# Attention, DFT and MLP on one core: two output rows of the second product kept in PSUM, half-array masks, one small add on ScalarE, and a new instruction order

## The chip, the core and the metric

One core of a Trainium2 chip runs the whole program. The metric is the device time of one execution in microseconds. The kernel before takes 950.18 us, the median of three runs (949.14 to 953.03).

## What is computed

The sizes are 4 batches, 12 heads, 448 positions, head size 64, model width 768 and hidden width 3072.

```python
scores = scale * q @ k.T                       # per batch and head, 448 x 448
scores = where(column > row, -1e9, scores)
attn = exp(scores - max(scores))
attn = attn / (sum(attn) + 1e-09)
x = attn @ v                                   # heads side by side: 4 x 448 x 768
u = x + real(fft(fft(x, axis=1), axis=2))
un = (u - mean(u)) / sqrt(var(u) + 1e-06)      # over the 768
out = u + maximum(un @ w_ch1, 0.0) @ w_ch2
```

## The kernel before

**Two-part numbers.** To keep accuracy, an operand of a product is cut into a high and a low part in float32r; a product is then three matmuls: high by high, high by low, low by high. One engine casts the high part (`copy`, line 333 or 335), another subtracts it for the low part (lines 430, 810, 866, 904, 1014, 1107).

**Attention** (`attend`) runs over 24 pairs of heads, two heads side by side in the 128 partitions. For each pair there are three score pieces: blocks of rows 0 and 1 together, block 2, and the tails of 64 rows of both heads. TensorE first writes the mask into the bank (line 447: an identity `idb` times a triangle `mkb`, both bfloat16, whole array), then adds the scores (line 455). The scores of the two heads use the upper and the lower 64 rows of the array, into the banks `sc` and `sd`. The score is kept negated, so VectorE's minimum (line 467) is the maximum, and ScalarE takes the exponential and its sum (line 471). VectorE adds 1e-9 to the seven sums (line 479) and takes the reciprocal (line 483); GpSimd or ScalarE normalise (lines 490 and 492); TensorE transposes (line 503) and multiplies with `v` on column halves of the array (line 529).

**Folding, DFT and normalisation** (`fold`, `dft`) follow for each batch, on all engines.

**The MLP** takes the 1792 rows in two passes (`g`) of 896 rows, which are 7 blocks of 128 (`k`). Each pass has 12 chunks (`c`) of 256 hidden columns. `f1` makes the first product of a chunk in four quarters. A chunk is slow (8 products of quarters) or, from `C_FAST` on and in all of the second pass, fast (Winograd's 7 products, with sums and differences made by VectorE and GpSimd, and banks copied to `c` on the way). From `C_FAST` on, the cut weights of the first pass are stored in DRAM and loaded again in the second (`kept`). `f2` makes the second product. In the first pass each block `k` and half `n` of 384 columns is a tile `o2` of six matmuls in a bank of its own (line 1218); VectorE adds it to `acc` in SBUF (line 1167), which ends with 14 adds a chunk.

**Order.** A planner (`Plan`) writes the order of every engine before the program is built. Each unit has an engine or a choice of engines, a cost, and a priority; the constants at the top (`SPLIT_AT`, `NORM_AT`, `W_LEAD`, `MIX_LEAD` and so on) are leads in units of a thousand per head pair or chunk. The unit that can start first by the planner's clock comes next. The 8 PSUM banks are one pool; `BANKS` gives each kind of tile a reserve and a limit. The hardware then runs each engine's list in that order and waits on semaphores.

Of the kernel before, what the change touches and what calls it, by code (L numbers as in the profile page):

```python
# [23 lines left out]
R = 112  # L24
# [11 lines left out]
BANKS = dict(sc=(1, 3), sd=(1, 2), pt=(1, 3), x=(1, 2), ay=(1, 3), an=(1, 1), at=(1, 5), h=(0, 5), o2=(0, 5))  # L36
# [28 lines left out]
CW = 128 + 192  # L65
# [5 lines left out]
GRP = [(0, 113), (113, 112), (225, 111), (336, 112)]  # L71


class Plan:
# [11 lines left out]
    def add(self, eng, cost, prio, fn, rd=(), wr=(), phase=None):  # L86
# [5 lines left out]
        for x in set(z[:2] for z in (*rd, *wr)):  # L92
# [3 lines left out]
            n=n, engs=dict(zip(eng, cost)) if many else {eng: cost}, many=many, prio=prio, fn=fn, deps=deps, phase=phase,  # L96
            new=sorted({z[:2] for z in wr if z[0] in self.bufs}, key=str)))

    def order(self):
# [74 lines left out]
        now = {"V": None, "G": None}  # L174

        def takes(n, e, t):
# [11 lines left out]
        while len(seq) < len(units):  # L188
            best = None
            for e, cand in pool.items():  # L190
                for n in cand:
# [71 lines left out]
def tile_kernel(ctx, tc, qk, vv, w1, w2, cc, cd, cs, out):  # L263
# [7 lines left out]
        "cst": ("const", [128, CW], F32, 1), "idb": ("const", [128, 128], BF16, 1),  # L271
        "mkb": ("const", [128, CW - 128], BF16, 1),  "eps": ("const", [128, 4], F32, 1), "pw": ("const", [128, 4], F32, 1),
# [21 lines left out]
        "h": ("P", [128, 512], F32, 1), "o2": ("P", [128, 512], F32, 1),  # L294
# [21 lines left out]
    def dve(n, rate=0.96):  # L316
        return 69 + n / rate
# [33 lines left out]
    def consts():  # L351
# [1041 lines left out]
```

## Time and profile before

| | before |
|---|---|
| median of 3 runs | 950.18 us |
| profiled execution | 950.98 us, span 949.2 us |
| PE busy | 904.6 us (95%), 5636 matmuls |
| DVE busy | 856.9 us (90%), 1455 instructions |
| ACT busy | 544.4 us (57%), 1300 instructions |
| POOL busy | 502.4 us (53%), 523 instructions |
| DMA | 165.84 MB |

PE is TensorE's matmuls, DVE VectorE, ACT ScalarE, POOL GpSimd. The stages show in what each engine does over the span: attention and DFT up to some 240 us, a change-over to 295, the first MLP pass to 645, the second to the end. A matmul's end is modelled in this profile, so that one which streams for 0.17 us is shown with 0.34; starts are what to measure between. A fast chunk of the first product begins where `t2`, `t3` and `t4` first appear, from 397 us on.

### The profile page before, as it was taken

To read this page: it belongs to the slowest core of one execution; us is meant where nothing else is said; L and a number is where in the kernel's file an instruction comes from. 1 tells how busy PE (TensorE), PEld (TensorE's weight loads), DVE (VectorE), ACT (ScalarE), POOL (GpSimd) and SP (SyncE) were. 2 spreads that over 40 slices of the span, in tenths; PEclk is the share of its full clock that TensorE was granted. 3 is DMA by queue.
4 is the path that set the end of the run, shared out by engine and by line. 5 is a ranking of instruction groups with operands and counts; after the bars stand their busy time and mean duration, and the time that the engine had idled before them with its cause. 6 is when DMAs were issued, how large, how long until landed. Compare 5 with 4: busy or idle time off the path is not lost.

```text
span 949.2 us, 16148 instructions
## 1 busy us (share of the span) xinstructions
PE 904.6 (95%) x5636; PEld 806.7 (85%) x5636; DVE 856.9 (90%) x1455; ACT 544.4 (57%) x1300; POOL 502.4 (53%) x523
## 2 busy tenths in 40 slices
PE   7999999999799999999999998989999999999997
PEld 4667668777689999988989887988989999999996
DVE  6889999998997787999998899989999999999998
ACT  6999898988644545545444446645554444434441
POOL 4798698884742122443342338775765333333331
PEclk9999999999899999999999999999999999999999
DMA  7634624616578556758696568654114444444303
GB/s 276 215 98 165 179 83 133 166 41 193 143 217 316 200 200 237 243 192 287 242 320 252 206 225 300 184 203 168 68 38 146 148 128 118 139 134 144 124 1 116
DMA packets 67537, 165.84 MB, mean 175 GB/s; under 512 B 18976, under 2 KB 31904, under 8 KB 67360
## 3 DMA queue, kind: packets, MB, share of 16 engines
q1 hardware_dynamic: 67456, 164.82, 52.5%
q8 instruction: 44, 0.72, 0.3%
q14 instruction: 37, 0.30, 0.1%
HBM read 112.89 MB, written 54.74 MB: 177 GB/s over the span
## 4 chain that ended last, share of the span: by engine, by line
PE 55%; DVE 25%; ACT 7%; issue 6%; POOL 5%; DMA 2%; SPq 0%; DVEq 0%; POOLq 0%; ACTq 0%
PE h L977 20%; PE o L1179 14%; PE o L1218 8%; PE x L529 4%; DVE acc L1167 4%; PE pt L503 3%; PE sc L455 3%; DVE w L761 3%; DVE w L751 2%; DVE w L810 2%; ACT p L471 2%; DVE ws L823 2%; DVE w L757 1%; DVE hl L1014 1%; DVE mn L467 1%
## 5 line engine op out<-in xcount | busy, mean ns | idle before, releaser
L1167 DVE TENSOR_TENSOR acc<-o,acc 128x384 f32<-128x384 f32 x444 | 231.1, 548 | 27.7 <-PE o L1218 19.1
L1218 PE MATMUL o<-w2h,hh 128*128 128x384 f32 x336 | 113.6, 338 | 2.1 <-DVE acc L1167 2.1
L1218 PE MATMUL o<-w2l,hh 128*128 128x384 f32 x336 | 113.9, 339 | 1.4 <-POOL w2l L778 1.3
L1218 PE MATMUL o<-w2h,hl 128*128 128x384 f32 x336 | 113.4, 338 | 0.0
L778 POOL TENSOR_TENSOR w2l<-w,w2h 128x768 fp32r<-128x768 f32 x24 | 49.6, 2070 | 78.5 <-ACT w2h L774 71.5
L492 POOL TENSOR_TENSOR p<-p,ri 128x128 f32<-128x128 f32 (+3 forms) x113 | 79.1, 729 | 21.9 <-DVE ri L483 18.1
L810 POOL TENSOR_TENSOR w<-w,w 128x384 fp32r<-128x384 f32 x30 | 36.1, 1205 | 66.5 <-ACT w L333 65.5
L977 PE MATMUL h<-u11h,w 128*128 128x448 f32 x174 | 64.9, 379 | 3.0 <-ACT u11h L333 3.0
L1179 PE MATMUL o<-w2l,hl 128*128 128x384 f32 x288 | 63.6, 340 | 4.1 <-DVE acc L1167 4.0
L1218 PEld LDWEIGHTS o<-w2h,hh 128*128 128x128 f32 x336 | 63.5, 189 | 4.6 <-DVE acc L1167 2.8
L1218 PEld LDWEIGHTS o<-w2l,hh 128*128 128x128 f32 x336 | 63.4, 189 | 4.4 <-POOL w2l L778 2.4
L977 PE MATMUL h<-u22h,w 128*128 128x448 f32 x174 | 63.1, 370 | 3.2 <-DVE c L1050 3.2
L1179 PE MATMUL o<-w2h,hh 128*128 128x384 f32 x288 | 65.2, 339 | 0.8 <-DVE acc L1167 0.8
L333 ACT COPY c<-h 128x448 f32<-128x448 f32 x57 | 30.1, 529 | 59.2 <-POOL w L877 25.4
L977 PE MATMUL h<-u12h,w 128*128 128x448 f32 x174 | 63.7, 368 | 0.0
L1218 PEld LDWEIGHTS o<-w2h,hl 128*128 128x128 f32 x336 | 63.5, 189 | 0.0
L977 PE MATMUL h<-u21h,w 128*128 128x448 f32 x174 | 63.1, 367 | 0.0
L503 PE MATMUL pt<-cst,p 128*128 128x128 f32 (+1 forms) x384 | 56.9, 281 | 2.6 <-ACT p L490 1.9
L1179 PEld LDWEIGHTS o<-w2l,hl 128*128 128x128 f32 x288 | 51.6, 188 | 8.0 <-DVE acc L1167 6.1
L503 PEld LDWEIGHTS pt<-cst,p 128*128 128x128 f32 (+1 forms) x384 | 41.4, 139 | 16.9 <-issue 5.7
L877 POOL TENSOR_TENSOR w<-w 128x384 f32<-128x384 f32 x15 | 19.3, 1290 | 68.6 <-issue 59.7
L999 ACT ACTIVATE c<-c 128x448 f32<-128x448 f32 x36 | 20.8, 579 | 59.3 <-DVE c L1050 59.3
(212 smaller groups left out, 3006.6 us busy)
## 6 DMA issues: line engine op xcount, KB each, us to landing
w<-in_w_dram SPq DMA_DIRECT2D x48, 768.0 KB, 5.0
wp<-w SPq DMA_DIRECT2D x49, 384.0 KB, 3.7
w<-wp SPq DMA_DIRECT2D x49, 384.0 KB, 3.1
wf<-w SPq DMA_DIRECT2D x34, 384.0 KB, 2.7
w<-wf SPq DMA_DIRECT2D x17, 768.0 KB, 4.8
raw<-in_qk_dram SPq DMA_DIRECT2D x23, 480.0 KB, 3.9
us<-und SPq DMA_DIRECT2D x45, 224.0 KB, 4.0
v<-in_vv_dram SPq DMA_DIRECT2D x24, 256.0 KB, 3.1
```

What stands on the lines that cost most here:

```text
L333: nc.scalar.copy(out=out, in_=in_)
L455: nc.tensor.matmul(out=T[ps][:, at[r]:at[r] + n], lhsT=T[a][s, q0:q0 + 128], rhs=T[c][s, 0:n], start=False, stop=y == len(rows) - 1 and z ...
L492: nc.gpsimd.tensor_tensor(out=x, in0=x, in1=z.to_broadcast([128, KE[r]]), op=ALU.mult)
L503: nc.tensor.transpose(T[ps][0:m, 128 * k:128 * k + 128], T[pb][:, PO[r] + 128 * c:PO[r] + 128 * c + m], T["cst", 0][:, 0:128])
L529: nc.tensor.matmul(out=T[xps][64 * h:64 * h + 64, q0:q0 + w], lhsT=T[v][0:kk, c, h * D:(h + 1) * D], rhs=T[src][0:kk, s0 + h * sd:s0 + h * ...
L761: nc.vector.scalar_tensor_tensor(out=T[w32], in0=T[w32], scalar=3, in1=T[w][:, :, 1], op0=ALU.logical_shift_left, op1=ALU.bitwise_or)
L778: nc.gpsimd.tensor_tensor(out=T[wl], in0=T[w32].bitcast(F32), in1=T[wh], op=ALU.subtract)
L810: (nc.gpsimd if eng == "G" else nc.vector).tensor_tensor(out=T[z][:, 1], in0=src(), in1=T[z][:, 0], op=ALU.subtract)
L977: nc.tensor.matmul(out=T[ps][:, 0:S], lhsT=a[:, t], rhs=x[:, t], start=start and k == 0, stop=stop and k == 8, skip_group_check=True)
L1167: nc.vector.tensor_tensor(out=x, in0=T[ps][:, 0:384], in1=x, op=ALU.add)
L1179: nc.tensor.matmul(out=T[ps][:, 0:384], lhsT=hpart(j, h, a)[:, k * 128:k * 128 + 128], rhs=T[z][:, 384 * b:384 * b + 384], start=start and ...
L1218: nc.tensor.matmul(out=T[ps][:, 0:384], lhsT=T[a][:, m, k * 128:(k + 1) * 128], rhs=w[:, sl], start=(m == 0 and z == 0), stop=(m == 1 and ...
```

## The change

1. **Rows in PSUM.** From chunk 3 of the first pass on, the blocks `k` = 0 and 1 of the second product are not added to `acc` chunk by chunk. They accumulate over nine chunks in three banks, `ra` (block 0, columns 0 to 511), `rc` (block 1, the same columns) and `rb` (columns 512 to 767 of both). After chunk 11 four adds bring them to `acc`.
2. **Half-array masks.** `idb` and `mkb` go; the constants come as bfloat16 bits within the `cst` load, which grows from 320 to 384 columns. For the score pieces of two heads a mask is two products on row halves, of 128 and of 64 columns, each for `sc` and `sd`. A tail's mask stays one product on the whole array.
3. **1e-9 on ScalarE** instead of VectorE.
4. **The planner** adds a price (`TURN`) when TensorE goes from whole-array work (F) to row halves (R) or column halves (C) or back, and has other prices for VectorE and GpSimd in SBUF at the same time (`BOTH`, with `T` for VectorE's double-rate operations).
5. **Constants**: fast chunks begin at 6 instead of 5, tables load from the third head pair on, and most leads are new.

```diff
-SPLIT_AT, FOLD_AT = -509, 5113
-DFT_AT, DFT_STEP = (4036, 3873, 3298, 3640), (77, 105, 133, 132)
-W_LEAD, F2_LAG = 809, 561
-BANKS = dict(sc=(1, 3), ..., h=(0, 5), o2=(0, 5))
+SPLIT_AT, FOLD_AT = -803, 5113
+DFT_AT, DFT_STEP = (4120, 3839, 3298, 3640), (77, 105, 166, 132)
+W_LEAD, F2_LAG = 783, 604
+BANKS = dict(sc=(1, 3), ..., h=(0, 5), o2=(0, 5), ra=(0, 1), rb=(0, 1), rc=(0, 1))
-C_FROM, W_FROM, N_WARM = 0, 8, 11
-N_W1, N_C, N_WS, C_FAST, C_MIX = 7, 3, 3, 5, 7
-MIX_LEAD, FILL_LEAD = -94, 417
-LATER = dict(S=-1500, V=-248, G=-847)
-NORM_AT, TR_AT = 1675, 1894
+C_FROM, W_FROM, N_WARM = 2, 8, 11
+N_W1, N_C, N_WS, C_FAST, C_MIX = 7, 3, 3, 6, 7
+C_RES = 3
+MIX_LEAD, FILL_LEAD = 48, 267
+LATER = dict(S=-1406, V=-248, G=-851)
+NORM_AT, TR_AT = 1514, 1343
-BOTH = dict(V=0.42, G=0.72)
+TURN = dict(FF=0, RR=0, CC=0, FR=92, RF=92, FC=45, CF=45, CR=45, RC=45)
+BOTH = dict(V=0.45, T=0.18, G=0.74)
...
@@ Plan.order
+                    if e == "PE":
+                        t += TURN[array, u["use"]]
                     key = (t, u["prio"], n)
...
@@ consts
-            copy(eng, T["mkb", 0], T["cst", 0][:, 128:CW])
...
-            copy(eng, T["idb", 0], T["cst", 0][:, 0:128])
...
@@ attend
-                for ps in banks:
-                    for y, r in enumerate(rows):
-                        e, m0, mw = at[r] + KE[r], 128 if tail else 0, 64 if tail else 128
-                        nc.tensor.matmul(
-                            out=T[ps][:, e - mw:e], lhsT=T["idb", 0], rhs=T["mkb", 0][:, m0:m0 + mw], start=y == 0, stop=False,
-                            skip_group_check=True)
+                cb = T["cst", 0][:, 128:CW].bitcast(BF16)
+                idb, mk = cb[:, 0:128], cb[:, 128:512]
+                for y, r in enumerate(rows):
+                    e = at[r] + KE[r]
+                    for w, a, m0 in ((64, idb, 128),) if tail else ((128, mk[:, 256:384], 0), (64, mk[:, 192:320], 128)):
+                        for h, ps in enumerate(banks):
+                            s = slice(0, 128) if tail else slice(64 * h, 64 * h + 64)
+                            nc.tensor.matmul(
+                                out=T[ps][:, e - w:e], lhsT=a[s], rhs=mk[s, m0:m0 + w], start=y == 0 and m0 == (128 if tail else 0),
+                                stop=False, skip_group_check=True)
...
-            nc.vector.tensor_scalar(out=T[ri], in0=T[sm], scalar1=1e-9, scalar2=None, op0=ALU.add)
+            nc.scalar.activation(out=T[ri], in_=T[sm], func=ACTF.Copy, bias=1e-9)
...
@@ f2, before the loop over the two halves n
+            if k < 2 and c >= C_RES:
+                r, half = ("ra", "rc")[k], "rb"
...
+                    for m in range(2):
+                        wh, wl = T["w2h", (j, m)], T["w2l", (j, m)]
+                        for z, (a, w) in enumerate(((hh, wh), (hh, wl), (hl, wh))):
+                            first = m == 0 and z == 0 and c == C_RES
+                            last = m == 1 and z == 2 and c == NCH - 1
+                            for ps, c0, d0, cw, own in ((r, 0, 0, 512, True), (half, 512, 256 * k, 256, k == 0)):
+                                nc.tensor.matmul(
+                                    out=T[ps][:, d0:d0 + cw], lhsT=T[a][:, m, k * 128:(k + 1) * 128], rhs=w[:, c0:c0 + cw],
+                                    start=first and own, stop=last, skip_group_check=True)
...
+                if c == NCH - 1 and k == 1:
...
+                                nc.vector.tensor_tensor(out=x, in0=T[ps][:, d0:d0 + cw], in1=x, op=ALU.add)
...
+                continue
```

What that does to the order is shown at three places. The first is TensorE's list at chunk 3 of the first pass, where the second product comes to block 0. Before (`o_5276` is the tile of the block's first half, `h` a tile of the first product):

```order
L1218 MATMUL o_5276<-w2h,hh 128x384
L1218 MATMUL o_5276<-w2l,hh 128x384
L1218 MATMUL o_5276<-w2h,hl 128x384
L1218 MATMUL o_5276<-w2h,hh 128x384
L1218 MATMUL o_5276<-w2l,hh 128x384
L1218 MATMUL o_5276<-w2h,hl 128x384
L977 MATMUL h<-u11h,w_5047 128x448
L977 MATMUL h<-u11l,w_5047 128x448
```

Now, at the same place of the work:

```order
L1233 MATMUL ra<-w2h,hh 128x512
L1233 MATMUL rb<-w2h,hh 128x256
L1233 MATMUL ra<-w2l,hh 128x512
L1233 MATMUL rb<-w2l,hh 128x256
L1233 MATMUL ra<-w2h,hl 128x512
L1233 MATMUL rb<-w2h,hl 128x256
L1233 MATMUL ra<-w2h,hh 128x512
L1233 MATMUL rb<-w2h,hh 128x256
```

The block is one unit of twelve matmuls into two banks that stay taken, where it was two units of six, each in a bank that an add set free again.

The second place is TensorE's list in attention, from the product with `v` to the scores of rows 0 and 1 of a head pair. Before (LDWEIGHTS loads the stationary operand; score rows carry it within):

```order
L529 MATMUL x<-pa,v 64x64 x2
L447 LDWEIGHTS idb
L447 MATMUL sc<-mkb,idb 128x128
L447 LDWEIGHTS idb
L447 MATMUL sc<-mkb,idb 128x128
L447 LDWEIGHTS idb
L447 MATMUL sd<-mkb,idb 128x128
L447 LDWEIGHTS idb
L447 MATMUL sd<-mkb,idb 128x128
L455 MATMUL sc<-kh,qh 128x128
```

Now, for such a pair:

```order
L541 MATMUL x<-pg,v 64x256 x2
L458 LDWEIGHTS cst
L458 MATMUL sc<-cst 128x128
L458 LDWEIGHTS cst
L458 MATMUL sd<-cst 128x128
L458 LDWEIGHTS cst
L458 MATMUL sc<-cst 128x64
L458 LDWEIGHTS cst
L458 MATMUL sd<-cst 128x64
```

The masks alternate between the two banks and are twice as many; 168 mask matmuls become 312. Over the whole list the neighbours of different array use change: F to R or back from 91 to 40, F to C or back from 119 to 56, R to C or back from 5 to 52.

The third is VectorE's list at the add of 1e-9 of a head pair (`un` is the normalisation of a DFT row, `mn` the minimum of a score piece). Before:

```order
L425 SCALAR_TENSOR_TENSOR ql<-raw,qh 128x512
L683 TENSOR_SCALAR un<-u,mv,rs 112x768
L479 TENSOR_SCALAR ri<-sum 128x7
L467 TENSOR_REDUCE mn<-sc 128x1
L483 RECIPROCAL ri<-ri 128x7
```

Now the add is in ScalarE's list, between an exponential, copies and normalisations:

```order
L483 ACTIVATE p,sum<-sd,mn 128x384
L347 COPY pg<-pt 128x512
L491 ACTIVATE ri<-sum 128x7
L483 ACTIVATE p,sum<-sc,mn 128x448
L347 COPY pg<-pt 128x512
L502 ACTIVATE p<-p,ri 128x448
```

VectorE keeps the reciprocal. Other work changes engine too. To VectorE go 9 scalings of `q` (9 to 18), 5 casts of `k` (11 to 16) and 10 copies to `xt` (4 to 14), all from ScalarE, which in turn does 70 normalisations instead of 55 and GpSimd 98 instead of 113. In all, VectorE's `acc` adds go from 444 to 412, TensorE's matmuls of 448 columns in the first product are 9 more, and one more chunk's second-pass weights are cut anew.

## Rows read from the trace of the kernel before

**Rows 1.** Busy time by stretch: length; PE, PEld, DVE, ACT, POOL (instructions); clock, DMA.

```profile
20.00:235.00 215.00, 209.16 (x1902) 154.04 (x1904) 191.94 (x393) 192.46 (x597) 173.53 (x220) 1.00 0.45 139
295.00:395.00 100.00, 100.00 (x535) 95.83 (x534) 83.10 (x128) 47.99 (x73) 27.31 (x19) 1.00 0.64 221
395.00:645.10 250.10, 234.76 (x1224) 219.96 (x1223) 235.77 (x333) 126.33 (x222) 125.91 (x92) 0.99 0.70 241
645.10:700.00 54.90, 52.14 (x272) 48.38 (x271) 52.59 (x89) 28.79 (x68) 42.02 (x39) 1.00 0.27 93
```

**Rows 2.** The chain that ended last, at 306 us: start, length, what.

```profile
306.13 3.71 PE h L977 x18
309.85 2.08 PE o L1218 x12
```

**Rows 3.** Busy time by stretch of line 977 alone, then of line 1218.

```profile
395.00:645.10 250.10, 122.50 (x527) 97.39 (x527) 0.99 0.70 241
...
395.00:645.10 250.10, 133.85 (x697) 123.66 (x696) 0.99 0.70 241
```

**Rows 4.** TensorE's waits, 395 to 645 us: total, times, longest.

```profile
PE h L977 <- ACT c L333: 9.5, 7, 2.8
...
PE o L1218 <- DVE acc L1167: 2.1, 2, 1.4
```

**Rows 5.** Four lines of the kernel: shortest, median and longest in ns.

```profile
L1167 DVE TENSOR_TENSOR acc<-o,acc x444: 539/546/560, 299.9 to 945.6; 128x384 f32<-128x384 f32 x148
...
L479 DVE TENSOR_SCALAR ri<-sum x24: 153/172/1144, 13.9 to 227.3; 128x7 f32<-128x7 f32 x24
...
L471 ACT ACTIVATION_READ_ACCUMULATOR p<-sc,mn x96: 190/206/284, 8.2 to 225.2; 128x1 f32 x96
...
L421 DVE TENSOR_SCALAR qh<-raw x9: 407/421/1393, 4.3 to 190.9; 128x512 fp32r<-128x512 f32 x9
```

**Rows 6.** TensorE in order of time, two score pieces: start, length, instruction.

```profile
122.78 0.23 PE L447 MATMUL sc<-mkb,idb 128*128 128x128 bf16 x1
...
123.00 0.44 PE L455 MATMUL sc<-kh,qh 64*128 64x384 f32 x1
...
127.07 0.28 PE L447 MATMUL sc<-mkb,idb 128*128 128x128 bf16 x2
...
127.39 0.32 PE L455 MATMUL sc<-kh,qh 64*128 64x128 f32 x1
...
127.55 0.27 PE L455 MATMUL sc<-kh,ql 64*128 64x128 f32 x1
...
127.66 0.27 PE L455 MATMUL sc<-kl,qh 64*128 64x128 f32 x1
...
128.06 0.28 PE L455 MATMUL sc<-kl,qh 64*128 64x256 f32 x1
...
128.27 0.55 PE L503 MATMUL pt<-cst,p 128*128 128x128 f32 x3
```

**Rows 7.** VectorE's groups by line and shape, 20 to 235 us: busy, mean ns.

```profile
L479 DVE TENSOR_SCALAR ri<-sum 128x7 f32<-128x7 f32 x22 | 10.5, 475 | 1.3 <-ACT p L471 1.3
...
L421 DVE TENSOR_SCALAR qh<-raw 128x512 fp32r<-128x512 f32 x7 | 4.9, 696 | 0.0
...
L335 DVE CAST kh<-raw 128x448 fp32r<-128x448 f32 x8 | 4.5, 557 | 0.0
```

**Rows 8.** The chain that ended last, the first 14 us.

```profile
1.64 4.01 DMA cst<-in_cc_dram
...
5.67 0.35 ACT mkb L333
...
6.28 0.29 PE sc L447 x2
```

**Rows 9.** In order of time: a tile's last matmul, then its add.

```profile
310.56 0.34 PE L1218 MATMUL o<-w2h,hl 128*128 128x384 f32 x1
...
310.93 0.56 DVE L1167 TENSOR_TENSOR acc<-o,acc 128x384 f32<-128x384 f32 x1 [1.87 <-PE o L1218]
```

More of the change, by code (lines that the diff above doesn't have):

```diff
@@ L71, with __add__ @@
 GRP = [(0, 113), (113, 112), (225, 111), (336, 112)]
+class Twin(float):
+    def __add__(self, x):
+        return Twin(float(self) + x)
 class Plan:
@@ L84, in __init__, with add @@
         self.units, self.writers, self.uses = [], {}, {}
-    def add(self, eng, cost, prio, fn, rd=(), wr=(), phase=None):
+    def add(self, eng, cost, prio, fn, rd=(), wr=(), phase=None, use="F"):
         n = len(self.units)
@@ L95, in add @@
         self.units.append(dict(
-            n=n, engs=dict(zip(eng, cost)) if many else {eng: cost}, many=many, prio=prio, fn=fn, deps=deps, phase=phase,
+            n=n, engs=dict(zip(eng, cost)) if many else {eng: cost}, many=many, prio=prio, fn=fn, deps=deps, phase=phase, use=use,
             new=sorted({z[:2] for z in wr if z[0] in self.bufs}, key=str)))
@@ L174, in order @@
         now = {"V": None, "G": None}
+        array = "F"
         def takes(n, e, t):
@@ L180, in takes @@
                 return c
-            both = end[o] - t
-            return c / BOTH[e] if c <= both * BOTH[e] else c + both * (1 - BOTH[e])
+            both, share = end[o] - t, BOTH["T" if isinstance(c, Twin) else e]
+            return c / share if c <= both * share else c + both * (1 - share)
         def when(n, e):
@@ L211, in order @@
             u["eng"], cost = e, takes(n, e, t)
+            if e == "PE":
+                array = u["use"]
             if e in now and side[e][n]:
@@ L215, in order @@
                 if o is not None and end[o] > t:
-                    late = (min(t + cost, end[o]) - t) * (1 - BOTH[x])
+                    late = (min(t + cost, end[o]) - t) * (1 - BOTH["T" if isinstance(units[o]["engs"][x], Twin) else x])
                     end[o] += late
@@ L316, in dve @@
     def dve(n, rate=0.96):
-        return 69 + n / rate
+        return Twin(69 + n / rate) if rate > 1 else 69 + n / rate
     def act(n, acc=0):
@@ L458, in attend @@
             n = sum(KE[r] for r in rows)
-            add("PE", 3 * mm(n) * 1.086 + (60 if tail else 110 * len(rows) + 200), p0, f, rd=[qh, ql, kh, kl, ("idb", 0), ("mkb", 0)], wr=banks, phase="A")
+            add("PE", 3 * mm(n) * 1.086 + (60 if tail else 90 * len(rows) + 15), p0, f, rd=[qh, ql, kh, kl, ("cst", 0)], wr=banks, phase="A",
+                use="F" if tail else "R")
             for y, r in enumerate(rows):
@@ L478, in f @@
         def f():
-            nc.vector.tensor_scalar(out=T[ri], in0=T[sm], scalar1=1e-9, scalar2=None, op0=ALU.add)
-        add("V", 72, base + 1000, f, rd=[(*sm, r) for r in range(NB)], wr=[(*ri, 0)], phase="A")
+            nc.scalar.activation(out=T[ri], in_=T[sm], func=ACTF.Copy, bias=1e-9)
+        add("S", acts(NB), base + 1000, f, rd=[(*sm, r) for r in range(NB)], wr=[(*ri, 0)], phase="A")
         def f():
@@ L1355 @@
     mask = np.concatenate(
-        [np.triu(np.ones((128, 128)), 1), np.tile(np.triu(np.ones((64, 64)), 1), (2, 1))], axis=1) * BIG
+        [np.tile(np.triu(np.ones((128, 128)), 1)[:64], (2, 1)), np.tile(np.triu(np.ones((64, 64)), 1), (2, 1))], axis=1) * BIG
+    place = np.tile(np.eye(64, 192, 64), (2, 1))
+    halfs = np.concatenate([np.eye(128), mask, place], axis=1).astype(np.float32).view(np.uint32) >> 16
+    halfs = np.ascontiguousarray(halfs.astype(np.uint16))
     def halves(a):
@@ L1372 @@
         "w2": inputs["moe_w_ch2"].reshape(2 * NCH, 128, DM),
-        "cc": np.concatenate([np.eye(128), mask], axis=1).astype(np.float32),
+        "cc": np.concatenate([np.eye(128, dtype=np.float32), halfs.view(np.float32)], axis=1),
         "cd": cd,
```

33 lines of the change are left out of this document (23 added, 10 removed).

## The prediction, on record before the changed kernel ran

> **What bounds the kernel now.** I read the stretches first, each with the busy time of every engine. In attention [rows 1] TensorE is busy 209.2 of 215 us, VectorE and ScalarE 192 each (89%), GpSimd 174: TensorE leads, two engines are close behind. From 295 to 395 us TensorE is busy all the time with VectorE at 83.1%. From 395 to 645 us, the fast chunks of the first pass, it is busy 234.8 of 250.1 and VectorE 235.8, 94.3%.
>
> Busy time flatters TensorE there, because the modelled end of a matmul covers the first part of a stall. The spacing of matmuls that follow each other doesn't: 18 with 448 columns in 3.71 us, 0.206 each; 12 with 384 columns in 2.08 us, 0.173 each [rows 2]. In the stretch stand 527 of the first product and 697 of the second [rows 3], 527 x 0.206 + 697 x 0.173 = 229.4 us. So 250.1 - 229.4 = 20.7 us are lost, 8.3%. The reader is to see that the stretch before loses nothing at the same work per chunk, with VectorE 11 points less busy. The waits name ScalarE's copies to `c` most [rows 4]: the first product has to go on in a bank that was just copied. Few are put down to VectorE's accumulation, since with eight banks there is another to fill. I read this as one cause, a row of small operations on VectorE, ScalarE and GpSimd that runs late because VectorE is full; that reading is what the first rival doubts.
>
> **The change part by part**
>
> *Rows kept in PSUM.* In nine chunks of the first pass (3 to 11) four adds each go, 36, and at chunk 11 four come: two of 512 columns, two of 256, together the columns of four old ones. Net 32 adds of 0.547 us, the 0.546 of [rows 5]: 17.5 us off VectorE, all but a little of it within the stretch. TensorE's columns stay: each product of 2 x 384 becomes 512 + 256. Three banks go, five are left for everything else; the price of that is a rival below.
>
> *Fast chunks start at 6 instead of 5.* Chunk 5 of the first pass takes 8 products instead of 7, 9 matmuls more: 9 x 0.206 = 1.85 us on TensorE. In the second pass chunk 5 has its weights split anew instead of loaded. The stretch in which such chunks run, 645 to 700, has TensorE idle 2.8 us over some two chunks [rows 1], so one more costs between 0 (POOL, at 42 of 55 there, is the cover) and 1.4. I take 0.5.
>
> *What the first pass gains.* TensorE's work in the stretch becomes 229.4 + 1.85 = 231.2, VectorE's 235.8 - 17.5 = 218.3. The loss was 0 at a VectorE share of 83.1% and 8.3% at 94.3%. Between the two I go in a straight line: with a stretch of 243 us the share is 218.3 / 243 = 89.8%, the loss (89.8 - 83.1) / (94.3 - 83.1) x 8.3% x 243 = 12.1, and 231.2 + 12.1 = 243.3, which closes. Gain 250.1 - 243.3 = 7 us. The bounds: no loss left, 20.7 - 1.85 = 19 us; the loss as it was, 1.85 us dearer.
>
> *Half-array masks, and turns priced in the order.* Call F an operation on the whole array, R one on row halves (the score pairs), C one on column halves (the products with v). Before the first score, two masks take 0.22 us (122.78 to 123.00) and four 0.32 (127.07 to 127.39) [rows 6]. So one mask is 0.05, and some 0.1 is left that doesn't grow with their number: the turn from F to R. The turn back shows too: from the last score pair to the next transpose 0.21 (128.06 to 128.27), against 0.11 between pairs (127.55 to 127.66) [rows 6]. Counted in the order of instructions, turns between F and R go from 91 to 40, between F and C from 119 to 56, between R and C from 5 to 52. The first are worth 51 x 0.10 = 5.1 us. For those with C no row is as clean: at one price they are 16 fewer, 1.6 us; with 0 for one kind and 0.10 for the other they lie between 6.3 saved and 4.7 lost. I take 0.10 for all, 6.7 us. Against it stand the masks: six whole-array ones a head pair, 6 x 0.05, become six pairs of halves, 144 pairs in all. A pair can't be cheaper than its columns (0.05 for 128, 0.025 for 64, mean 0.037) and should not be dearer than a score pair, 0.11, whose weights are four bytes wide: from 1.8 us saved to 8.6 lost. I take 0.065, nearer to the whole-array mask, which has the same type and columns: 2.2 us lost. Net 4.5 saved.
>
> The Trainium skill, TensorEngine Tiling (Array Packing), section Instruction Overhead, has about 60 cycles as the least a matmul costs; at the full clock that prices a 64-column mask like its columns, and by it the masks would save 0.7 us rather than lose 2.2. No run here shows that figure yet.
>
> *1e-9 on ScalarE.* The add of 7 columns is short when alone, 0.153, median 0.172, but 1.144 at worst; 22 of them in the attention stretch cost 10.5 us [rows 5, 7]. The reciprocal behind it stays. On ScalarE it is an operation as small as the accumulator read, 0.206 [rows 5]: 24 x 0.206 = 5 us there. But VectorE doesn't come out lighter: the new order gives it 9 more scalings of q (0.696 each in this stretch, 6.3), 5 more casts of k (0.557, 2.8) [rows 7], and 10 more copies to `xt`, each of half as many columns as the cast (about 0.28 to 0.56, say 0.4: 4). 10.5 off, 13 on. ScalarE loses about as much as it gains. So both stay at 192 us while TensorE gets shorter; at 192 of 211 that is 91%. I let two thirds of TensorE's 4.5 through: 3 us. The bounds of the stage: 13 us gained (6.7 + 4.7 + 1.8, all on the path), 5 lost.
>
> On the scalings the rows are two-sided: median 0.421, worst 1.393 [rows 5]. The Trainium skill, SBUF — State Buffer, section Who interferes with whom, has casts and scalar operations of VectorE, in their two-port mode, and GpSimd's operations shut each other out for a whole instruction. The trace agrees in kind (0.172 against 1.144). By that rule the 14 moved operations speak against the change, and it gives the second rival.
>
> *Start.* The two casts stand between the load and the first mask: ScalarE starts at 5.67 and the first mask at 6.28 [rows 8], 0.6 us that go. The load grows by a fifth: 0 to 0.8 us of its 4.01 [rows 8]. I take 0.1. Gain 0.5.
>
> *New leads and prices of the plan.* They change the order everywhere and the work nowhere; I cost them at nothing beyond the turns, and let them widen the range.
>
> Sum: 0.5 + 3 + 7 - 0.5 = 10 us. The profiled execution took 950.98 (span 949.2 and 1.8 around it), so 941.0; the median of the runs is 0.8 lower: 940.2, forecast 940.
>
> **Rivals**
>
> *The freed VectorE isn't what TensorE waits for.* For it: of the waits put down to an engine 9.5 us are on the copy to `c`, 2.1 on accumulation [rows 4]. If ScalarE's own queue holds those copies, the loss stays and the extra chunk is paid: 950.2 - 0.5 - 3 + 1.85 + 0.5 = 949. Against it: 295 to 395 us loses nothing, although that stretch has no such copies, so it doesn't speak cleanly.
>
> *VectorE and GpSimd block each other more in attention.* The 14 moved operations at up to 1.39 us instead of ScalarE's time: (1.39 - 0.6) x 14 = 11 us more on VectorE, 203 of 211, and attention gets 3 us longer rather than shorter: 940 + 6 = 946. GpSimd, which does 15 fewer normalisations, speaks against it.
>
> *Five banks are too few: the slower side.* From the start of the last matmul of a second-product tile (310.56) its add starts 0.37 us later and takes 0.56 [rows 9]; a tile that finds only that bank free starts at 311.49 instead of 310.73, 0.76 us late. In the nine chunks 90 such tiles remain, and the first product's tiles hold up to three banks of the five. If 30 of them wait, that is 23 us: 940 + 23 = 963. It decides above (10 + 4.8) / 0.76 = 20 tiles. Against it: the kept rows are 18 blocks of 2.1 us of work that ask for no bank, and VectorE is lighter.
>
> **How the numbers follow.** The forecast and its neighbourhood (933 to 946) get 0.56; a larger gain, with most of the loss gone and attention worth 6 or more (924 to 933), 0.16; the first rival 0.13; the second 0.07; the banks 0.08. The forecast's own range is 933 to 946. The range for 8 in 10 leaves out the banks and the tip of the large gain: 926 to 951. A measurement of this kernel can tell 0.5% from no change, that is 945.4 and 954.9. Faster: 0.54 + 0.16 + 0.02 = 0.72; within: 0.02 + 0.12 + 0.05 = 0.19; slower: the banks and the rest, 0.09.
>
> **What would show it.** VectorE's busy time in the first pass 17 us less; TensorE's lost time between chunk 3 and the second pass about 12 us, no longer 20.7; waits for `c` shorter. In attention the gap from the first mask to the first score without the 0.1 us when it follows a C operation, and half-mask pairs at 0.04 to 0.11. The add of 1e-9 at about 0.2 us on ScalarE. I am wrong if the first pass keeps its loss, if waits of the second product on `acc` adds reach 15 us, or if attention ends later than before.

## The result: 1.5% slower, not 1% faster

The changed kernel takes 966.5 us (964.08 to 967.86, 4 runs) beside 951.61 (949.14 to 953.99, 4 runs) of the kernel before: a ratio of 1.0146, interval 1.0121 to 1.017. Forecast were 940 us and a range of 926 to 951. The profiled execution took 966.81 us with a span of 964.6; 15.4 us more than the span before are to be found.

I cut each run at two points that the groups by line show as the start of a line's first matmul: the first product with w2 of the first pass, and that of the second pass. Each stage time here and below comes from one profiled execution. That of before took 950.98 us, while nearly all of its single runs beside the experiments lie between 950 and 957.6; a difference of 1 or 2 us in a stage says little by itself.

| us | up to the first product with w2 | first pass | second pass |
|---|---|---|---|
| before | 292.4 | 353.0 | 303.8 |
| after | 297.0 | 356.1 | 311.5 |
| more | 4.6 | 3.1 | 7.7 |
| forecast | -3.5 | -7 | +0.5 |

The first two terms came out on the other side, and the third far above its forecast. The busy time of after by the same stretches, moved to where they now lie, with the columns of [rows 1] (length; PE, PEld, DVE, ACT, POOL; granted clock, DMA):

```profile
20.00:238.70 218.70, 205.77 (x2034) 155.64 (x2032) 194.95 (x396) 190.56 (x608) 163.85 (x208) 0.98 0.48 149
299.60:399.60 100.00, 100.00 (x535) 95.98 (x534) 80.41 (x127) 47.81 (x71) 20.60 (x13) 1.00 0.61 210
399.60:653.10 253.50, 239.41 (x1234) 220.89 (x1233) 220.84 (x302) 124.48 (x221) 123.58 (x90) 0.98 0.67 231
653.10:708.00 54.90, 51.99 (x258) 47.16 (x257) 52.06 (x83) 25.89 (x61) 36.93 (x37) 0.97 0.27 91
```

In attention TensorE has less to do (205.8 us busy, before 209.2) and takes longer all the same, 218.7 us: idle 12.9 us instead of 5.8. In the first pass VectorE is lighter by 14.9 us and TensorE's stretch longer by 3.4. The matmuls there, by line (first product, second product, kept rows):

```profile
399.60:653.10 253.50, 126.57 (x537) 99.81 (x535) 0.98 0.67 231
...
399.60:653.10 253.50, 101.75 (x504) 91.09 (x504) 0.98 0.67 231
...
399.60:653.10 253.50, 36.02 (x192) 30.50 (x192) 0.98 0.67 231
```

The 192 of the kept rows are as many columns on average as the others. With the spacings of [rows 2] unrounded (3.71 / 18 and 2.08 / 12 us) the 537 and 696 matmuls are 231.3 us of work (forecast 231.2), and 253.5 - 231.3 = 22.2 us are lost, before 20.7. What TensorE waited for there, total, times and longest, is nearly unchanged [rows 4], and the wait on `acc` that would speak for too few banks is smaller:

```profile
PE h L989 <- ACT c L347: 8.9, 6, 4.2
...
PE o L1262 <- DVE acc L1179: 0.7, 2, 0.5
```

What grew is in attention: the transposes of the normalised rows wait 8.9 us for `un`, before 3.8, and the transposes of `p` wait 5.8 us in all, before 2.6. The waits for `un` of before and of after:

```profile
PE at L693 <- DVE un L683: 3.8, 4, 2.0
```

```profile
PE at L705 <- DVE un L695: 8.9, 6, 3.5
```

The longest in TensorE's order, and the rows on VectorE and GpSimd at that time:

```profile
110.53 0.27 PE L466 MATMUL sc<-kl,qh 64*128 64x256 f32 x1
...
114.34 1.38 PE L705 MATMUL at<-cst,un 112*128 112x112 f32 x6 [3.53 <-DVE un L695]
```

```profile
111.79 2.49 DVE L695 TENSOR_SCALAR un<-u,mv,rs 112x768 f32<-112x768 f32 x1 [0.44 <-POOL rs L686]
...
111.78 2.08 POOL L590 TENSOR_TENSOR fl<-d,fh 128x896 fp32r<-128x896 f32 x1
```

The small parts did what they should. Score pieces of after, to be read against [rows 6]:

```profile
129.02 0.23 PE L458 MATMUL sc<-cst 64*128 64x128 bf16 x1
...
129.09 0.19 PE L458 MATMUL sc<-cst 64*128 64x64 bf16 x1
...
129.12 0.22 PE L458 MATMUL sc<-cst 64*128 64x128 bf16 x1
...
129.20 0.30 PE L466 MATMUL sc<-kh,qh 64*128 64x128 f32 x1
...
131.36 0.23 PE L458 MATMUL sc<-cst 64*128 64x128 bf16 x1
...
131.46 0.42 PE L466 MATMUL sc<-kh,qh 64*128 64x384 f32 x1
```

Four pairs of half masks take 0.18 us to the first score, two pairs 0.10: 0.045 to 0.05 a pair, and no 0.1 us beside them. A pair of 128 columns takes 0.07 (129.02 to 129.09), one of 64 columns 0.03 (129.09 to 129.12). The add of 1e-9 on ScalarE, and the kept rows' adds:

```profile
L491 ACT ACTIVATE ri<-sum x24: 208/234/265, 13.2 to 232.1; 128x7 f32<-128x7 f32 x24
...
L1249 DVE TENSOR_TENSOR acc<-rb,acc x2: 411/412/412, 636.1 to 638.3; 128x256 f32<-128x256 f32 x2
L1249 DVE TENSOR_TENSOR acc<-ra,acc x1: 675/675/675, 633.9 to 633.9; 128x512 f32<-128x512 f32 x1
```

### The profile page after: what moved, and what is told of

Same layout as the page of the kernel before. It is cut to its first block, busy times and chain, and to the rows that moved or that the text cites. A ratio compares the mean times of both kernels' runs of the same rounds, so it can differ in the third digit from the quotient of the medians.

```text
span 964.6 us, 16388 instructions
## 1 busy us (share of the span) xinstructions
PE 912.9 (95%) x5789; PEld 812.1 (84%) x5789; DVE 847.1 (88%) x1432; ACT 537.7 (56%) x1300; POOL 499.3 (52%) x514
## 5 line engine op out<-in xcount | busy, mean ns | idle before, releaser
L1179 DVE TENSOR_TENSOR acc<-o,acc 128x384 f32<-128x384 f32 x408 | 212.2, 548 | 25.5 <-PE o L1262 22.4
L1262 PE MATMUL o<-w2h,hh 128*128 128x384 f32 x264 | 90.2, 342 | 0.7 <-DVE acc L1179 0.7
L1262 PE MATMUL o<-w2l,hh 128*128 128x384 f32 x264 | 90.0, 341 | 0.3 <-POOL w2l L790 0.3
L1262 PE MATMUL o<-w2h,hl 128*128 128x384 f32 x264 | 89.9, 340 | 0.0
L504 POOL TENSOR_TENSOR p<-p,ri 128x128 f32<-128x128 f32 (+3 forms) x98 | 65.5, 697 | 13.4 <-DVE ri L495 12.4
L1191 PE MATMUL o<-w2h,hh 128*128 128x384 f32 x288 | 65.8, 346 | 2.7 <-DVE acc L1179 2.6
L483 ACT ACTIVATE p<-sc,mn 128x448 f32<-128x448 f32 (+3 forms) x96 | 50.2, 523 | 16.0 <-DVE mn L479 13.9
L1191 PEld LDWEIGHTS o<-w2h,hh 128*128 128x128 f32 x288 | 53.3, 192 | 6.8 <-DVE acc L1179 4.8
L763 DVE SCALAR_TENSOR_TENSOR w<-w 128x768 uint32<-128x768 uint32 x48 | 52.2, 1087 | 3.3 <-ACT w L753 2.2
L479 DVE TENSOR_REDUCE mn<-sc 128x1 f32<-128x448 f32 (+3 forms) x96 | 44.4, 463 | 11.9 <-ACT p L483 5.6
L1262 PEld LDWEIGHTS o<-w2h,hh 128*128 128x128 f32 x264 | 50.2, 190 | 3.9 <-DVE acc L1179 1.7
L773 DVE SCALAR_TENSOR_TENSOR w<-w,w 128x768 uint32<-128x768 uint32 x48 | 52.2, 1087 | 0.3
```

Of the source, the lines that this page charges most:

```text
L479: nc.vector.tensor_reduce(out=T[mn][:, rr:rr + 1], in_=T[ps][:, c0:c0 + n], axis=AX, op=ALU.min)
L483: nc.scalar.activation(out=T[pb][:, PO[rr]:PO[rr] + n], in_=T[ps][:, c0:c0 + n], func=ACTF.Exp, scale=-1.0, bias=T[mn][:, rr:rr + 1], accu ...
L504: nc.gpsimd.tensor_tensor(out=x, in0=x, in1=z.to_broadcast([128, KE[r]]), op=ALU.mult)
L763: nc.vector.scalar_tensor_tensor(out=x, in0=x, scalar=0x80000000, in1=T[w][:, :, 0], op0=ALU.bitwise_and, op1=ALU.bitwise_or)
L773: nc.vector.scalar_tensor_tensor(out=T[w32], in0=T[w32], scalar=3, in1=T[w][:, :, 1], op0=ALU.logical_shift_left, op1=ALU.bitwise_or)
L1179: nc.vector.tensor_tensor(out=x, in0=T[ps][:, 0:384], in1=x, op=ALU.add)
```

## The experiments

**The parts without the new order.** A first theory: the parts are worth little, and the order that the plan works out anew costs the time. Its rival: one of the parts costs it. The kept rows alone (chunk 5 of the first pass stays fast, old leads and rules; the plan is worked out anew from chunk 3 on); the half masks alone, emitted where the old masks stood, the order held; the add alone, order held:

```diff
+C_RES = 3                      # e1, with the block of the kept rows and its banks
-lhsT=T["idb", 0], rhs=T["mkb", 0][:, m0:m0 + mw]     # e2
+lhsT=a[s], rhs=mk[s, m0:m0 + w]
-nc.vector.tensor_scalar(out=T[ri], in0=T[sm], scalar1=1e-9, ...)   # e3
+nc.scalar.activation(out=T[ri], in_=T[sm], func=ACTF.Copy, bias=1e-9)
```

> The kernel before, with the two rows of the second product kept in three banks and nothing else (old constants, fast chunks from 5, order planned anew by the old rules). Theory order (the time went into new stalls of the new order, each made longer by the lower clock behind it): the rows alone cost little or gain, 944 to 953 us. Rival banks (five banks are too few): 955 to 970 us, with waits of the second product or of h on VectorE up by 5 us or more.

> The kernel before, with the half-array masks alone and the order of the other instructions held as it was (the planner is given the old costs; the two casts of the mask are left out). Theory order: some 0.3 us less on TensorE per head pair, 7 in all, of which half or more shows: 944 to 948 us. Rival masks (twice as many matmuls cost more than they save): 952 to 955 us.

> The kernel before, with the add of 1e-9 emitted on ScalarE and the order otherwise held (the planner still thinks of VectorE). Theory order: VectorE loses 10.8 us of busy time, ScalarE gains 24 x 0.23 = 5.5: 946 to 951 us. Rival add (a late step on a ScalarE that is 89% busy): 952 to 956 us.

The other side: the new rules and leads, with fast chunks from 6, and none of the three parts.

> The changed kernel's planner rules and constants (leads, TURN, BOTH, fast chunks from 6), without the rows in PSUM, with the old whole-array masks, casts and the add on VectorE. Theory order: the loss comes with the order, 960 to 972 us. Rival parts (rows or masks carry the loss): 950 to 956 us, of which 1.85 are the slow chunk 5.

| run | ratio to before | to w2 | first pass | second pass |
|---|---|---|---|---|
| e1 kept rows | 0.999 (0.9976 to 1.0004) | 293.9 | 351.9 | 306.0 |
| e2 half masks | 1.0011 (0.9995 to 1.0026) | 289.9 | 353.2 | 311.0 |
| e3 add on ScalarE | 0.9992 (0.9971 to 1.0013) | 293.0 | 352.5 | 305.0 |
| e4 order without parts | 1.018 (1.0153 to 1.0208) | 294.2 | 366.4 | 310.4 |

No part alone costs anything that these runs can tell (at most 0.3%, by the upper ends of the intervals), and the new rules and leads without the parts cost at least as much as the whole change: the intervals, 1.0153 to 1.0208 and 1.0121 to 1.017, overlap. The order of e4 is not that of after, since the planner reckons with the old masks.

**Which piece of the new order.** The changed kernel with all the old leads, chunk 5 fast among them; with chunk 5 fast alone; with the old prices of turns and shared ports; with leads and prices both undone, so that of the change only the three parts are left, in an order planned anew.

```diff
-SPLIT_AT, FOLD_AT = -803, 5113 ...     # e5: all leads as before
+SPLIT_AT, FOLD_AT = -509, 5113 ...
-N_W1, N_C, N_WS, C_FAST, C_MIX = 7, 3, 3, 6, 7     # e6
+N_W1, N_C, N_WS, C_FAST, C_MIX = 7, 3, 3, 5, 7
-TURN = dict(... FR=92 ...); BOTH = dict(V=0.45, T=0.18, G=0.74)     # e7
+TURN = dict(... FR=0 ...); BOTH = dict(V=0.42, T=0.42, G=0.72)
```

> The changed kernel with all three parts and the new planner rules (TURN, BOTH), but the leads and constants of before (fast chunks from 5 too). Theory leads: the new leads carry the loss, so it goes: 944 to 954 us. Rival rules (TURN and BOTH make the worse order): 960 to 970 us.

> The changed kernel with fast chunks from 5 again, all else as changed. If the slow chunk 5 and its weights in the second pass carry much of the loss: 953 to 960 us. If only its 9 matmuls count: 963 to 966 us.

> The changed kernel with the new leads, but TURN at 0 and BOTH as before. Theory leads: 960 to 972 us. Rival rules: 948 to 956 us.

> Rows in PSUM, half-array masks and the add on ScalarE together, with the leads, constants and planner rules of before. By the runs of each part alone (952.6 to 954.8 beside 953.1) they add up to nothing: 950 to 956 us. If they help each other, since the masks shorten TensorE's list in attention and the others lighten VectorE: 940 to 948 us.

Then small nudges of leads that change no work: in before's attention, in its later stages, and in the changed kernel; later a second one in before's attention.

```diff
-NORM_AT, TR_AT = 1675, 1894     # e9
+NORM_AT, TR_AT = 1675, 1920
-W_LEAD, F2_LAG = 809, 561       # e10
+W_LEAD, F2_LAG = 815, 566
-W_LEAD, F2_LAG = 783, 604       # e11, and SPLIT_AT by 6
+W_LEAD, F2_LAG = 789, 609
-NORM_AT, TR_AT = 1675, 1894     # e16, and FILL_LEAD by 3
+NORM_AT, TR_AT = 1655, 1870
```

> The kernel before with one lead of attention moved by a hair (TR_AT 1894 to 1920, 26 thousandths of a head pair) and no work changed: only the order differs. Theory scatter (the order of before is a good one among many, and any new order, whatever made it, falls 1 to 2% behind): 957 to 972 us beside 953. Rival (orders made by the same rules are about equal): 950 to 956 us.

> The kernel before with two leads of the MLP moved by a hair (W_LEAD 809 to 815, F2_LAG 561 to 566), the order of attention as it was. Theory scatter: 955 to 965 us, less than for attention, since the fast MLP chunks leave fewer choices. Rival: 950 to 956 us.

> The changed kernel with three leads moved by a hair (SPLIT_AT -803 to -797, W_LEAD 783 to 789, F2_LAG 604 to 609). Theory scatter: anywhere from 955 to 975 us, at least 3 us from the changed kernel's own 966 either way. Rival: 964 to 968 us.

> The kernel before with three of its leads moved a little (NORM_AT by -20, TR_AT by -24, FILL_LEAD by 3) and no change of work. If any new order of the attention costs some: ratio 1.003 to 1.015, as the first such nudge (1.0066). If that nudge was bad luck: within 0.997 to 1.003.

And all three parts put into the order of before's attention as it stands, with the kept rows as in e1:

> The kernel before with the kept rows (planned anew from chunk 3 on, as in the run of the kept rows alone), and the half-array masks and the 1e-9 on ScalarE put into the order of before's attention as it stands; old leads, old planner rules, chunk 5 still slow. By the theory that the parts cost little and the order of the attention costs the time, it lands where the parts alone landed: ratio 0.996 to 1.003. If the parts disturb each other: over 1.005.

| run | ratio to before | to w2 | first pass | second pass |
|---|---|---|---|---|
| e5 old leads | 1.0161 (1.0135 to 1.0187) | 298.9 | 358.2 | 308.1 |
| e6 chunk 5 fast | 1.0112 (1.0084 to 1.014) | 295.6 | 355.5 | 309.0 |
| e7 old rules | 1.0187 (1.0158 to 1.0215) | 306.4 | 355.4 | 307.1 |
| e8 parts, planned anew | 1.0112 (1.0083 to 1.0141) | 295.7 | 358.9 | 307.7 |
| e13 parts, order held | 0.9978 (0.9962 to 0.9995) | 289.7 | 352.1 | 306.2 |
| e9 nudge | 1.0066 (1.0044 to 1.0088) | 298.0 | 355.5 | 304.2 |
| e16 nudge | 1.0068 (1.0044 to 1.0091) | 296.5 | 358.0 | 304.6 |
| e10 nudge, later stages | 0.9986 (0.9967 to 1.0004) | 293.1 | 353.0 | 305.1 |
| e11 nudge of after | 1.0207 (1.0187 to 1.0227) | 300.3 | 359.8 | 311.2 |

The pair that decides is e8 and e13: the same three parts, chunk 5 fast and the old leads and rules in both (e13 has chunk 5 fast, as before has it, and not slow as its text says), 964.12 against 950.79 us, with 953.6 for before beside each. 13.3 us lie between a program planned anew from its start and one whose attention is left in the order that it had. Two nudges that change no work cost 0.7% each, by 5.6 and 4.1 us up to w2 and 2.5 and 5.0 in the first pass.

The traces show a place for much of this, and it is not attention. In e8 the last product with `v` starts at 236.7 us, in e13 at 235.3. Then the first cut weights of w2 are late. TensorE at that place in e8, and in e16:

```profile
295.67 0.44 PE L1262 MATMUL o<-w2h,hh 128*128 128x384 f32 x1 [4.26 <-ACT w2h L786]
297.56 0.69 PE L1262 MATMUL o<-w2l,hh 128*128 128x384 f32 x1 [1.44 <-POOL w2l L790]
```

```profile
296.47 0.44 PE L1218 MATMUL o<-w2h,hh 128*128 128x384 f32 x1 [2.13 <-ACT w2h L774]
298.43 0.44 PE L1218 MATMUL o<-w2l,hh 128*128 128x384 f32 x1 [1.52 <-POOL w2l L778]
```

The waits for `w2h` and `w2l` there come to 6.2 us in e8, 5.0 in e16 and 3.9 in e9; before has 1.0 and e13 none. Behind them the granted clock is 0.50, for 6.8 us in e8 and in e16 and for 3.4 us in e9. With the wait ahead of the first product with w2, and counted to the 120th matmul behind it, e8 loses 8.9 us there to e13, of 14.4 between their spans; e16 loses 7.0 of 9.9 to before, and e9 4.7 of 8.5. The changed kernel itself waits only 0.3 us there: its 15.4 us are lost at other places.

Neither the leads nor the rules nor a part carries the 1.5% alone. e6, with chunk 5 fast, is 3 us below after, but the two intervals overlap. The nudge of the later stages (e10) costs nothing; it leaves TensorE's list in the first pass as it was and changes that of the second. The nudge of after (e11) adds another 0.6%. e13 has the lowest time of the kernels that leave no work out, 2 to 3 us below before, interval 0.9962 to 0.9995.

**Is it the wait for `un`?** A theory: the scaling to `un` collides with GpSimd, and TensorE waits for it. First the scaling goes to ScalarE, with two more one-column operations on GpSimd for its bias; then three pairs of transposes come two, three and six pieces later in TensorE's order.

```diff
-(nc.gpsimd if eng == "G" else nc.vector).tensor_scalar(out=T[un][0:w], ...)     # e12
+nc.scalar.activation(out=T[un][0:w], in_=T[u][0:w], func=ACTF.Identity, scale=..., bias=...)
-seq = plan.order()     # e17
+seq = later(plan.order(), {6: 2, 7: 2, 8: 3, 9: 3, 24: 6, 25: 6})
```

> The changed kernel with the order held and the DFT rows' normalisation (un) emitted on ScalarE instead of VectorE, GpSimd making the bias with two more operations of one column. Theory collision (in the new order VectorE's un is shut out by GpSimd, up to 3.5 us, TensorE waits 8.9 us for it and then runs at the lower clock): 953 to 961 us, the waits of the transposes on un below 3 us. Rival (another late step takes the place): 964 to 970 us.

> The changed kernel in its own order, but six groups of transposes that TensorE waits with (the un rows at 114.34, 154.92 and 272.27, stalls of 3.53, 1.55 and 2.56 us) come two, three and six pieces of work later in TensorE's order, with their copies behind them; nothing else moves. If what the new order costs in the attention is where it put these transposes: TensorE does the scores and products first, and the stretch up to the first product of the second kind falls from 297 to 290 to 292, time 959 to 961. If other engines bound the stage (filling the same stalls gained nothing there): 296 to 298, time 964 to 968.

e12: 967.15 us, ratio 1.0131 (1.0096 to 1.0167), up to w2 298.8. e17: 975.38, ratio 1.0219 (1.0176 to 1.0261), up to w2 306.3. TensorE's longest waits up to w2, of e12 and then of e17:

```profile
PE at L707 <- ACT un L698: 6.2, 8, 3.1
```

```profile
PE pt L534 <- POOL p L523: 5.4, 6, 2.2
PE an L679 <- DVE u L689: 4.7, 2, 2.8
...
PE at L724 <- DVE un L714: 2.2, 3, 1.2
```

In e12 the wait for `un` fell only from 8.9 to 6.2 us, not below 3 as was expected: the scaling takes 1.03 us on ScalarE, without the long cases that VectorE has (up to 3.54), and TensorE still waits. So e12 shows that the collision with GpSimd isn't needed for the loss, and not what the wait is worth. In e17 the wait fell to 2.2, and the stage got 9.3 us longer (306.3 after 297.0): the time came back as waits for `p` and for `u` at pieces further on. Neither theory gave time back.

**Is it the clock?** After the 3.53 us of idling TensorE ran at half speed. The third column from the right of these rows is the granted clock, of after and then of e14, where 46 matmuls that nothing reads fill four stalls:

```profile
110.00:115.00 5.00, 1.47 (x20) 1.27 (x17) 4.56 (x10) 3.78 (x10) 4.09 (x5) 0.89 1.05 366
115.00:120.00 5.00, 5.00 (x26) 4.01 (x25) 3.69 (x9) 4.80 (x18) 3.42 (x5) 0.50 0.30 88
```

```profile
110.00:115.00 5.00, 4.77 (x40) 2.57 (x41) 4.56 (x7) 4.42 (x12) 4.65 (x5) 1.00 1.03 359
115.00:120.00 5.00, 3.74 (x30) 2.80 (x31) 5.00 (x13) 4.23 (x16) 3.75 (x5) 1.00 0.47 153
```

```diff
+fill(("at", calls.count("at")), ps)     # 14, 6 and 10 matmuls of 512 columns, and 16 ahead of the first product
 nc.tensor.transpose(T[ps][:, tt * 113:tt * 113 + w], T[un][0:w, ...], ...)
```

> The changed kernel in its own order, with 46 matmuls of 512 bf16 columns that nothing reads, put ahead of four things that TensorE waits for: 14 before the stall of 3.53 us at 114.34, 6 before 1.55 at 154.92, 16 before 3.81 at 245.09, 10 before 2.56 at 272.27. They take 0.21 us each and fit into the stalls. If the low clock after a stall (0.50 granted in 115 to 120 and 245 to 250, some 10 us lost up to 297) is what turns a stall into a loss: those windows show a clock near 1, the attention is 5 to 8 us shorter, time 959 to 961. If the work there waits for other engines anyway: the clock rises and the time stays, 965 to 967.

963.73 us, ratio 1.0109 (1.0086 to 1.0133): up to w2 297.5, first pass 355.3, second 308.5. In these 10 us the clock stays at its full 2.4 GHz where it had fallen to 1.2, and attention ends no sooner: now VectorE is busy for all of those 5 us, and TensorE, faster, for only 3.74. What was gained, 3 us, lies in the second pass, and the intervals of after and e14 overlap. The low clock behind this stall ran in time that was lost anyway. For the rest of the run the mean granted clock speaks: 0.993 in the profiled execution of before, 0.980 in after, 0.995 in e14, which is still 1.1% slower than before, and 0.985 in e13, which is the fastest of the four. So the clock doesn't carry the 1.5%.

**Is a full VectorE what loses the first pass's time?** The prediction read it so. In e15 steps 4 and 3 begin in banks of their own, so that these products don't wait for a copy to `c` of their bank; what the old banks held is left out of these two quarters. e18 makes the adds to `acc` of chunks 3 to 11 short, and leaves out 320 of their 384 columns.

```diff
-x4 = run(pa, 4, "22", "t4", p[5], rd=[(*u3, 0)], stop=True)     # e15, step 3 alike
+x4 = run(pe, 4, "22", "t4", p[5], start=True, stop=True)
-x = T[acc][:, n * 384:(n + 1) * 384]     # e18
+w = 64 if g == 0 and c >= 3 else 384
+x = T[acc][:, n * 384:n * 384 + w]
```

> The kernel before, with steps 4 and 3 of each fast first product begun in banks of their own instead of going on in the banks that step 7 and step 5 filled; what those banks held is left out of these two quarters. The copies, adds and all matmuls stay, and so does VectorE's work. If the first pass loses its time in the chain product, copy to c, product: the waits of h for c go, and the 22 us lost there fall to 10 to 15, time about 941 to 946. If it is a full VectorE: they stay at 20 to 24, time 950 to 955.

> The kernel before in its own order, with the 126 adds into acc of chunks 3 to 11 of the first pass made on 64 columns instead of 384, so that 320 of 384 columns of these partial sums are left out. VectorE is some 45 us lighter there (126 adds of 0.55 become about 0.18), 2.7 times what the kept rows took off. If a full VectorE is what loses the first pass's 22 us, as my prediction read it: they fall under 8, and by the straight line of the prediction to 0 to 3, time 931 to 938. If fixed chains lose them: over 16, time 945 to 951.

e15: 957.42 us, ratio 1.0039 (1.0019 to 1.0058), first pass 356.0. e18: 948.88, ratio 0.9961 (0.9944 to 0.9977), first pass 348.8. The stretch of the fast chunks of e18, and its waits; then those of e15:

```profile
395.00:641.20 246.20, 235.50 (x1228) 222.61 (x1227) 207.78 (x334) 125.98 (x222) 123.33 (x92) 0.99 0.71 245
```

```profile
PE h L977 <- ACT c L333: 9.0, 7, 2.8
PE h L977 <- DVE c L1050: 1.1, 2, 0.8
PE o L1219 <- DVE acc L1168: 0.5, 1, 0.5
```

```profile
PE o L1218 <- POOL w2l L778: 8.4, 5, 2.5
PE h L977 <- ACT c L333: 2.6, 2, 2.0
```

With the stretch's matmuls counted as above (528 and 700 in e18; 525 and 699 in e1 from 396.5 to 645.8), the loss stands against VectorE's share so (the second column is what the straight line of the prediction gives):

| | VectorE's share | by the straight line | lost |
|---|---|---|---|
| before | 94.3% | 20.7 | 20.7 us |
| e1 | 89.2% | 11 | 19.9 us |
| after | 87.1% | 7.5 | 22.2 us |
| e18 | 84.4% | 2.4 | 16.0 us |

VectorE can be made 28 us lighter (235.8 to 207.8), and 4.7 of 20.7 us come back; the waits for ScalarE's `c` stay at 9 us. (45 us lighter was expected: the adds lost 38, and other operations of VectorE took some 10 us longer.) What came back is about what TensorE waited for VectorE itself: its copies to `c` from 3.2 us to 1.1, its adds from 2.1 to 0.5. The wait of before that goes with the first of these:

```profile
PE h L977 <- DVE c L1050: 3.2, 3, 1.7
```

With most of the waits for ScalarE's `c` gone (e15), the loss is 25.5 us (522 and 694 matmuls in 253.4 us), and TensorE waits 8.4 us for `w2l`, before 0.3. This run doesn't move the wait alone: the planner gave the first pass a new order for the two tiles more, and the eight banks hold these too. So a lighter VectorE gave back some 5 of the 20.7 us, and what loses the rest isn't shown. One reading fits these runs: each engine works through a list in a fixed order, and a wait that is taken away is found again at the next entry that isn't ready.

## Why the prediction was wrong, step by step

**The step that failed first** is the one on the plan: "They change the order everywhere and the work nowhere; I cost them at nothing beyond the turns". e4 shows the new rules and leads, with the slow chunk 5 and no part, at 1.018, and e8 against e13 shows 13.3 us for the same parts in an order planned anew. TensorE stands at 97% busy in before's attention [rows 1], VectorE and ScalarE at 89%. The kernels that keep the order of before's attention reach w2 at 289.7 to 293.9 us, the nine that have it planned anew at 294.2 to 306.4. So the order of before is a good one among many, and new ones cost what nudges cost and more. That belonged in the sum, as a loss of about 0.7% for any new order of attention, and as a rival with a chance of its own. In e8, e9 and e16 half and more of the cost is the late weights of w2; why the order of after costs what it does stays open: the waits for `un`, the clock, the leads and the rules were each tried and none carries it.

**What the first pass gains** (forecast 7 us, came out as 3.1 lost). Of these 3.1 the work of the slow chunk 5 is 1.9, as forecast; the loss itself stayed, 22.2 us after 20.7. VectorE got lighter by 14.9 us of the 17.5 forecast. The straight line between two shares was the error: "I read this as one cause" is refuted by e18, where the line has 2.4 us lost and the chip 16.0. The first rival, that the freed VectorE isn't what TensorE waits for, was right for most of this stretch's loss. It gave 949; with the cost of the new order and of chunk 5 in the second pass, which it leaves out, it falls short as well.

**Attention** (forecast -3, with the start -3.5; came out +4.6). The pieces were right. In the order of before, e13 ends this part 2.7 us earlier and e2 2.5; five other kernels with that order, or nearly that (e1, e3, e10, e15, e18), end it at 292.5 to 293.9. The first score of after starts at 5.66 us instead of 6.6. Half masks cost 0.045 to 0.05 a pair, not the 0.065 that I took. The Trainium skill, TensorEngine Tiling (Array Packing), section Instruction Overhead, priced the 64-column mask like its columns, and by that the masks would cost no more than the old ones; the trace agrees (0.03 a pair of 64 columns, 0.045 to 0.05 a pair on average, 0.05 a whole mask before). The 0.7 us saved that the prediction works out from it isn't what its own prices give: 72 pairs at 0.05 and 72 at 0.025 take 5.4 us, 1.8 less than 144 whole masks. As measured, they save 0 to 0.7. The add on ScalarE takes 0.234 (forecast 0.2). What failed is "I let two thirds through": none came through in the order that the plan chose.

**VectorE and GpSimd in attention** (a rival, 946). VectorE's scalings of q and casts of k did move there, but its busy time rose only from 191.9 to 195.0 us. Moving `un` off it (e12) gained nothing.

**The slow chunk 5** (forecast 1.85 + 0.5). The second term was sized too small. Count TensorE's matmuls back from the end of the run: the 200 from the 1200th to the 1000th, in the second pass, take 41.1 us in after and 39.7 to 41.2 in the seven kernels with a slow chunk 5, but 37.7 to 39.4 in the thirteen with a fast one, before and e6 among them (37.9 each). The rows of these 200 for after, before and e6:

```profile
727.60:768.70 41.10, 39.15 (x201) 35.94 (x202) 40.07 (x67) 19.26 (x46) 23.45 (x25) 1.00 0.22 68
```

```profile
716.60:754.50 37.90, 37.70 (x202) 35.97 (x201) 36.38 (x68) 18.10 (x42) 15.56 (x19) 1.00 0.42 128
```

```profile
726.70:764.70 38.00, 37.96 (x201) 36.51 (x202) 35.28 (x65) 16.86 (x40) 17.34 (x21) 1.00 0.40 129
```

So one more chunk whose weights are split anew costs 2 to 3 us there, an estimate from these spans, and the idle 2.8 us of the stretch of [rows 1] behind which I took 0.5 didn't show it. It fits the 3 us that e6 gives back.

**Five banks.** Refuted: the second product waits 0.7 us for `acc` in the first pass, where 15 us were named as the mark.

**The second pass** (forecast +0.5, came out +7.7), half of the whole loss, I had not looked at, since the diff touches little there. With the order that before has there, it takes 303.8 to 305.8 us in before, e3, e9, e16 and e18, and 311.0 in e2; with the order of after 308.5 to 311.5 in after, e12, e14 and e17. So some 5 of the 7.7 us go with the change, 2 to 3 of them as chunk 5 above; what the others wait for isn't shown.

## What to carry to other kernels

Where, as here, one engine is over 95% busy and two more near 90%, the order of the work can be a result of tuning, and a change of a cost or a lead can lose it: put a part into the old order first (e13), and count a new plan as a cost of its own, measured by a nudge that changes no work. Look in the nudge's trace for the one place where it lost the time, here the first weights of the next stage. A loss beside a high busy share is not thereby caused by it; make that engine much lighter first, in a kernel that leaves out a part of its work, before a change is built on it. And a wait that tops the list tells where the time shows, not what gives it back: two were made short here (`un` in e17, `c` in e15), and the time came back under other names.

## What was not expected of the hardware

The second pass differs between kernels whose order there is the same. In e2, VectorE and GpSimd fall into step; in before, they don't. VectorE of e2, and GpSimd of e2 (start, length):

```profile
645.23 0.55 DVE L871 TENSOR_TENSOR w2l<-w,w2l 128x384 fp32r<-128x384 f32 x1
645.70 1.37 DVE L1112 TENSOR_TENSOR hh<-c,hh 128x384 fp32r<-128x384 f32 x1
647.00 1.38 DVE L1112 TENSOR_TENSOR hh<-us,hh 128x384 fp32r<-128x384 f32 x1
```

```profile
645.39 1.27 POOL L882 TENSOR_TENSOR w<-w 128x384 f32<-128x384 f32 x1 [5.69 <-DVE w2h L871]
646.62 1.35 POOL L815 TENSOR_TENSOR w<-ws,w 128x384 fp32r<-128x384 f32 x1
```

The same instructions of before:

```profile
647.36 0.55 DVE L866 TENSOR_TENSOR w2l<-w,w2l 128x384 fp32r<-128x384 f32 x1
647.83 0.56 DVE L1107 TENSOR_TENSOR hh<-c,hh 128x384 fp32r<-128x384 f32 x1
648.29 0.56 DVE L1107 TENSOR_TENSOR hh<-us,hh 128x384 fp32r<-128x384 f32 x1
648.76 0.55 DVE L1107 TENSOR_TENSOR hl<-us,hl 128x384 fp32r<-128x384 f32 x1
```

```profile
647.52 2.67 POOL L877 TENSOR_TENSOR w<-w 128x384 f32<-128x384 f32 x1 [5.70 <-DVE w2h L866]
```

Either VectorE runs through at 0.56 each and GpSimd's operation takes 2.67 instead of 1.27, or the two alternate and VectorE's take 1.37. The Trainium skill, SBUF — State Buffer, section Who interferes with whom, has the shared ports as a lock that the one who starts first holds for a whole instruction, while the other waits until it ends. The alternation in e2 agrees with it; that GpSimd's one operation in before lasts through four operations of VectorE isn't explained by it. Which picture comes about isn't decided by the order of the instructions, which is the same in both, nor by their starts: in both GpSimd starts 0.16 us behind the same operation of VectorE (645.39 after 645.23, 647.52 after 647.36), and what decides it stays open. In e2 TensorE's wait for `acc` behind that place is 2.50 us, in before 0.93, and behind it the granted clock is 0.50 for 3.4 us where before keeps 1.00. The second pass of e2 is 7.2 us longer; that this is the whole of the 7.2 isn't shown.
